# Attention and two expert layers on one core: the second batch's scores in one-head float32r tiles

## The chip, the cores and the metric

The kernel runs on one core of a Trainium2 chip. The metric is the device time of one execution in microseconds, as the median of the runs; three runs of the kernel before stand at 1053.46, 1054.71 and 1057.16 us. A core has TensorE (PE, which multiplies matrices; its weight loads are listed as PEld), VectorE (DVE), ScalarE (ACT), GpSimd (POOL) and SyncE (SP), which here issues all transfers. Each engine works through its own instructions in order.

## The reference

The inputs q, k and v have the shape 4 batches x 8 heads x 576 positions x 64. A query sees the keys of its own block of 64 positions and of earlier blocks:

```python
scores = scale * np.matmul(q, k.transpose(0, 1, 3, 2))
mask = block_i >= block_j
scores = np.where(mask, scores, -1000000000.0)
scores = scores - np.max(scores, axis=-1, keepdims=True)
attn = np.exp(scores)
attn = attn / (np.sum(attn, axis=-1, keepdims=True) + 1e-09)
return np.matmul(attn, v).astype(np.float32)
...
x = np.ascontiguousarray(attn_out.transpose(0, 2, 1, 3)).reshape(B * S, H * D)
a, b = x @ w_a, x @ w_b          # first layer, 2304 x 512 by 512 x 1536
x = a * b @ w_out
xn = x / np.sqrt(np.mean(x * x, axis=-1, keepdims=True) + 1e-06) * rms_g
g = xn @ w_gate                  # second layer
out = g / (1 + np.exp(-g)) * (xn @ w_val) @ w_out
```

The three weight matrices of each layer come as 64-bit floats and are turned into pairs of 32-bit numbers on the core.

## The kernel before, in words

The heads are worked in 16 pairs, m = 0 to 15, four pairs a batch. Each pair has two parts, its first six query blocks of 64 and its last three. In each part `score` makes the score tiles, their maximum (DVE, L480 to L484) and their exponential (ACT, L486), and then the scaling by the sum (POOL, L498). `p_transposes` turns the scaled tiles (PE L523; ACT L525 and DVE L529 take them out of PSUM), and `values` or, for the first batch, `whole_values` multiplies with v (PE L592 or L548).

There are two forms of score tile, chosen by `single(m)`. The old form takes 64 queries of both heads of a pair as 128 rows, against the keys of both heads, in plain float32 (L457, two recorded instructions for each). The new form (L465) takes 128 queries of one head. Query and key are split in a rounded part and a remainder, float32r; the keys' two parts lie above one another in the 128 rows, so one matmul with the rounded queries (`qh`) and one with their remainders (`ql`) do all the products. The last 64 queries of both heads share the tile `qe`. In that form `make_q` does the split (ACT L111 the rounding, POOL L121 the remainder), `make_k` scales and splits the keys (ACT L411, DVE L413), and a DVE memset (L467) masks a 64x64 corner of each tile. Before the change `SINGLE = 2`: pairs 8 to 15 (third and fourth batch) have the new form, pairs 0 to 7 the old one.

The buffers of the two forms overlap. The raw queries of the new form lie in the buffer of the old form's even pairs (`qz0`), the remainders in that of the odd pairs (`qz1`), and the rounded queries in the two `x` buffers of the weight decoding.

The first layer runs over blocks of 512, 256, 512 and 1024 tokens, the second over three blocks of 768. While the first block runs, the first layer's weights are decoded: a piece is loaded (SP L190), taken apart (ACT L146 and L149, DVE L152, POOL L153), and split in two float32r parts (ACT L111; DVE or POOL L121). Three of five pieces lie in the slots `ld`, two in `st`. Attention of the next batch runs beside each block of the first layer; how far it may go is set by the cost that each step yields, against that of the main products, times `PACE`. The scheduler of the framework then puts each engine's instructions in an order by priority and by its own forecast of times.

In the second layer each product is made from seven smaller ones over three blocks of the ring `w`; ACT copies of PSUM (L743, L862) stand between one product and the next. Beside a block runs the normalisation of the next one, `normed`: the load of x2 (L1006), its squares (ACT L1009 and L1011), the mean by a matmul with ones, the factors and the scaling (DVE L1044), then the sums and splits that the next block multiplies. `before_fc` advances it by one step for each of the 24 steps of a block.

Of the kernel before, what the change touches and what calls it, by code (L numbers as in the profile page):

```python
# [9 lines left out]
F32R = mybir.dt.float32r  # L10
# [6 lines left out]
P = 128  # L17
# [10 lines left out]

WHOLE = 1

SINGLE, MASKED = 2, -1e30

RING = 19
UNSCALE = 2.0 ** -8
# [17 lines left out]
def tile_attention_moe_moe(  # L52
# [15 lines left out]
    B, H, D, S = q.shape  # L68
# [22 lines left out]
    stage = staging.enter_context(tc.tile_pool(name="stage", bufs=2))  # L91
# [24 lines left out]
    def split(hi, lo, src, eng_hi, eng_lo, late=None):  # L116

        ins = copy(eng_hi, hi, src)
        if eng_hi is act and late is not None:
            behind(ins, late)  # L120
        eng_lo.tensor_tensor(lo, src, hi.bitcast(F32), ALU.subtract)  # L121
        return ins
# [34 lines left out]
    w_pieces = []  # L157
# [13 lines left out]
    LANDING, landing = 5, []  # L171
    staged, prepared, wtiles = {}, [0], {}

    def stage_loads(n):
        while len(staged) + prepared[0] < min(n, len(w_pieces)):
            i = len(staged) + prepared[0]
            layer, kind, f, y = w_pieces[i]
            if layer == 0 and i % LANDING < LANDING - 2:
                if not landing:
                    landing.append(stage.tile([P, LANDING - 2, 4 * P], I64, tag="bg", name="ld", bufs=1))  # L180
                st = landing[0][:, i % LANDING]
            else:
                st = stage.tile([P, 4 * P], I64, tag="st", name="st", bufs=2)
            if kind == "o" and layer == 1:

                for dm in range(KC):
                    z, o = divmod(dm * TF + f % TF, KC)
                    sp.dma_start(out=st[:, dm * P:dm * P + P], in_=w_o[1][f // TF, z, :, o * P:o * P + P])
            else:
                sp.dma_start(out=st, in_=(w_ab if kind == "ab" else w_o)[layer][f, y])  # L190
            staged[i] = st

    def prepare():

        i = prepared[0]
        if i >= len(w_pieces):
            return
        stage_loads(min(i + min(2 + i, LANDING), max(len(w_pieces) // 2, i + 2)))
        layer, kind, f, y = w_pieces[i]
        w = 4 * P  # L200
        if layer == 0:
            if y == 0:
                if kind == "ab":
                    wtiles["ab", f] = wab.tile([P, 4, KC * P], F32R, tag="ab", name="ab")
                else:
                    wtiles["o", f] = wop.tile([P, 2, TF * DM], F32R, tag="o", name="o")
            t = wtiles[kind, f]
            dst = t[:, 2 * y:2 * y + 2, :] if kind == "ab" else t[:, :, y * w:(y + 1) * w]
        else:
            if f % 2 == 0:  # L210
                quarters["src"] = stage.tile([P, 8, 2 * P], F32, tag="src", name="src", bufs=1)
            src = quarters["src"]
            if kind == "ab":
                at = (0, 6)[f % 2]
                place = src[:, at:at + 2, :]
            else:
                place = src[:, f % 2:f % 2 + 7:6, :]
            decode(staged.pop(i), place)
            prepared[0] += 1
            if f % 2 == 1:  # L220
                combine(wc_dram[f // 2][y] if kind == "ab" else wco_dram[f // 2], src)
            return
        x = decode(staged.pop(i)).rearrange("p a b -> p (a b)")
        prepared[0] += 1
        split(dst[:, 0, :], dst[:, 1, :], x, act, eng[W_LO[i % len(W_LO)]], "act")
        if y == (1 if kind == "ab" else TF - 1):
            sp.dma_start(out=wab_dram[f] if kind == "ab" else wo_dram[f], in_=t.bitcast(F32))
# [20 lines left out]
    def fetch_ab(n):  # L248
        t = wtiles["ab", n] = wab.tile([P, 4, KC * P], F32R, tag="ab", name="ab")
        sp.dma_start(out=t.bitcast(F32), in_=wab_dram[n])  # L250

    def fetch_o(i):
        t = wtiles["o", i] = wop.tile([P, 2, TF * DM], F32R, tag="o", name="o")
        sp.dma_start(out=t.bitcast(F32), in_=wo_dram[i])
# [55 lines left out]
    def attention(pools, x_of, done):  # L310
# [20 lines left out]
        MAIN = S - Q  # L331
        q_raw, q_hi, q_lo = {}, {}, {}

        FIRST_SINGLE = SINGLE * (H // 2)

        def single(m):
            return m >= FIRST_SINGLE
# [93 lines left out]
        def make_q(m, part):  # L431
            if m >= NP or not single(m):
                return
            if not q_hi:
                assert prepared[0] >= len(w_pieces) // 2
                for hh in range(2):
                    q_hi[hh] = stage.tile([P, MAIN], F32R, tag="x", name="qh", bufs=2)
                t = ap.tile([P, 2 * MAIN + 3 * Q], F32R, tag="qz1", name="ql")
                for hh in range(2):
                    q_lo[hh] = t[:, hh * MAIN:(hh + 1) * MAIN]  # L440
                for x, end in ((q_hi, ap.tile([P, 3 * Q], F32R, name="qe")), (q_lo, t[:, 2 * MAIN:])):
                    act.activation(end[:, Q:2 * Q], pp[NQ - 1][:, S:S + Q], AF.Copy)
                    x["end"] = end
            a, z = (PARTS[0][0] * Q, PARTS[0][-1] * Q + Q) if part == 0 else (PARTS[1][0] * Q, MAIN)
            todo = [(q_hi[hh][:, a:z], q_lo[hh][:, a:z], q_raw[m][:, hh, a:z]) for hh in range(2)]
            if part == 1:
                ends = [x["end"].rearrange("p (t q) -> p t q", t=3)[:, 0:3:2] for x in (q_hi, q_lo)]
                todo.append((*ends, q_raw[m][:, :, MAIN:]))
            for hi, lo, raw in todo:
                split(hi, lo, raw, act, pool)  # L450
            if part == 1:
                load_q(m + 1)
# [162 lines left out]
        for u in range(2 * NP + 2):  # L615
            m, part = divmod(u, 2)
            if u >= 2:
                yield from (whole_values if (u - 2) // H < WHOLE else values)(u - 2)
            sc = list(SCORED[part]) if m < NP else []
            ct = p_transposes(u - 1) if 1 <= u <= 2 * NP else iter(())  # L620
            if sc:
                yield score(m, sc.pop(0))
                if len(sc) > 2:
                    yield score(m, sc.pop(0))
                if part == 0:
                    make_vv(m)
                    make_q(m, 1)
                else:
                    make_k(m + 1)
                    if m + 1 > FIRST_SINGLE:  # L630
                        make_q(m + 1, 0)
            alive = True
            while sc or alive:
                c = next(ct, None) if alive else None
                if c is None:
                    alive = False
                else:
                    yield c
                if sc:
                    yield score(m, sc.pop(0))  # L640
            if m < NP and part == 1:
                if m + 1 == FIRST_SINGLE:
                    make_q(m + 1, 0)
                load(m + 2)

# [413 lines left out]
    for at, (layer, t0, n_tok, parts) in enumerate(blocks):  # L1059
# [10 lines left out]
        if layer == 0:  # L1070
            acc = [accs.tile([P, KC, BMAX[0]], F32, tag="acc", name="acc")]
            for o, n in parts[1:]:
                nxt.append(split_of(t0 + o, n, True))
                acc.append(xs.tile([P, KC, S], F32, tag="xf", name="acc", bufs=2))
                t = xs.tile([P, KC, S], F32R, tag="xf", name="h", bufs=2)
# [16 lines left out]
        def before_fc(fc, n_tiles=n_tiles, at=at, layer=layer, following=following, norm=norm, got=got):  # L1092
            if at == 0:
                if fc > 0:
                    for _ in range(TF):
                        if prepared[0] < len(w_pieces) // 2:
                            prepare()
            elif layer == 0:
                if fc % TF == 0:
                    fetch_o(fc // TF)  # L1100
                if fc + 2 < FC:
                    fetch_ab(fc + 2)
                n = sum(BACKGROUND[:at]) + min(BACKGROUND[at], BACKGROUND[at] * (fc + 1) // (FC - 3))
                while prepared[0] < len(w_pieces) // 2 + n:
                    prepare()
                if prepared[0] == len(w_pieces) and not rings:
                    staging.close()
                    rings.append(ctx.enter_context(tc.tile_pool(name="ring", bufs=RING, side="right")))
                    fetch_to(RING - 1)
            if following and following[0] == 0 and fc + 2 >= FC:  # L1110
                fetch_ab(fc + 2 - FC)
            if fc > 0:
                for _ in range(FC * 2 // n_tiles):
                    if layer == 0 and len(got.get("x") or ()) == len(EARLY):
                        break
                    got["x"] = next(norm, None) or got.get("x")
# [100 lines left out]
```

## Time and profile before

| | us |
|---|---|
| median of 3 runs | 1054.71 |
| the profiled execution | 1053.99 |
| its span, first to last instruction | 1052.0 |
| PE busy | 1037.8 |
| DVE busy | 702.6 |
| ACT busy | 619.0 |
| POOL busy | 423.5 |

The span is that of the profiled execution; the rest of its time lies before the first and behind the last instruction. A busy PE is not a PE at its peak: the recorded duration of a matmul reaches over the start of the next, so for the cost of one the distance between two starts is the better measure. Idle time counts only where it ends up on the path to the last instruction.

### The profile page before, as it was taken

The page shows a single profiled execution, that of the slowest core. Times are in us where ns is not written, and L with a number is a line of the kernel's source. Part 1 is how long each engine was busy: PE and PEld are TensorE (multiplying, and loading weights), DVE is VectorE, ACT ScalarE, POOL GpSimd, SP SyncE. Part 2 cuts the span into 40 slices and gives each one's busy share as a digit, 9 for nine tenths or more (in the row PEclk, how much of TensorE's full clock was granted, in tenths as well). Part 3 has the DMA queues.
Part 4 walks back from the last instruction along what each step waited for, and adds up shares of the span by engine and source line. Part 5 has one row for each costly group of instructions (what it writes and reads, how often), then busy time and mean ns, then how long its engine had stood idle before and what let it go on. Part 6 is the DMA issues. An engine that isn't in the chain of part 4 may idle for free.

```text
span 1052.0 us, 16959 instructions
## 1 busy us (share of the span) xinstructions
PE 1037.8 (99%) x5676; PEld 934.4 (89%) x5676; DVE 702.6 (67%) x1371; ACT 619.0 (59%) x1376; POOL 423.5 (40%) x448
## 2 busy tenths in 40 slices
PE   9989999999999999999999999999999999999998
PEld 6768877899998888888888888999999999999998
DVE  5546767677766777676687734784876838666285
ACT  7868968667656766556544323653656536355362
POOL 5855766546564655455554501120221202212020
PEclk9999999999999999999999999999999999999999
DMA  9865978889997765788989665787789888887883
GB/s 242 232 202 194 294 258 300 313 270 290 347 371 261 270 223 210 288 330 313 340 312 349 255 225 181 216 284 258 242 301 302 275 268 251 294 265 240 266 247 116
DMA packets 116380, 281.25 MB, mean 267 GB/s; under 512 B 27971, under 2 KB 40771, under 8 KB 105798
## 3 DMA queue, kind: packets, MB, share of 16 engines
q1 hardware_dynamic: 116294, 280.18, 79.8%
q8 instruction: 45, 0.74, 0.3%
q14 instruction: 41, 0.34, 0.1%
HBM read 218.77 MB, written 61.36 MB: 266 GB/s over the span
## 4 chain that ended last, share of the span: by engine, by line
PE 85%; ACT 4%; DMA 4%; DVE 2%; POOL 2%; SPq 1%; issue 1%; POOLq 0%; ACTq 0%
PE mm L735 25%; PE mm L766 12%; PE mm L707 8%; PE mm L708 8%; PE mm L709 8%; PE mm L667 4%; PE mm L668 4%; PE mm L669 4%; PE t L592 3%; PE t L523 3%; PE s L465 3%; PE t L548 1%; DMA st<-in_w_o_dram 1%; POOL x L153 1%; PE s L457 1%
## 5 line engine op out<-in xcount | busy, mean ns | idle before, releaser
L708 PE MATMUL mm<-xl,ab 128*128 128x512 f32 (+1 forms) x480 | 180.8, 377 | 0.0
L707 PE MATMUL mm<-xh,ab 128*128 128x512 f32 (+1 forms) x480 | 179.8, 377 | 0.0
L709 PE MATMUL mm<-xh,ab 128*128 128x512 f32 (+1 forms) x480 | 179.4, 374 | 0.0
L735 PE MATMUL mm<-hT,w 128*128 128x384 f32 x576 | 165.5, 337 | 1.3 <-ACT mm L743 1.3
L121 POOL TENSOR_TENSOR hl<-g,hh 128x384 fp32r<-128x384 f32 x36 | 42.7, 1186 | 298.7 <-ACT hh L111 298.7
L735 PE MATMUL mm<-hB,w 128*128 128x384 f32 x432 | 125.9, 336 | 0.0
L766 PE MATMUL mm<-hh,w 128*128 128x384 f32 x504 | 125.2, 336 | 0.0
L743 ACT ACTIVATE mm<-mm 128x384 f32<-128x384 f32 x144 | 66.8, 474 | 75.5 <-PE mm L735 39.3
L735 PEld LDWEIGHTS mm<-hT,w 128*128 128x128 f32 x576 | 105.9, 188 | 2.7 <-ACT mm L743 2.4
L709 PEld LDWEIGHTS mm<-xh,ab 128*128 128x128 f32 x480 | 90.5, 189 | 15.2 <-issue 0.5
L707 PEld LDWEIGHTS mm<-xh,ab 128*128 128x128 f32 x480 | 90.4, 188 | 15.1 <-issue 0.2
L708 PEld LDWEIGHTS mm<-xl,ab 128*128 128x128 f32 x480 | 90.5, 189 | 14.8 <-issue 0.2
L498 POOL TENSOR_SCALAR pp<-pp,st 128x256 f32<-128x256 f32 (+4 forms) x144 | 83.3, 592 | 50.0 <-DVE st L495 35.5
L735 PE MATMUL mm<-lT,w 128*128 128x384 f32 x288 | 96.9, 337 | 0.0
L486 ACT ACTIVATE pp<-s,st 128x288 f32<-128x288 f32 (+8 forms) x142 | 72.0, 510 | 33.0 <-DVE st L480 16.2
L766 PEld LDWEIGHTS mm<-hh,w 128*128 128x128 f32 x504 | 90.6, 188 | 0.3 <-ACT mm L743 0.3
L766 PE MATMUL mm<-hl,w 128*128 128x384 f32 x252 | 81.4, 336 | 0.0
L735 PEld LDWEIGHTS mm<-hB,w 128*128 128x128 f32 x432 | 79.5, 188 | 0.0
L667 PE MATMUL mm<-hh,o 128*128 128x512 f32 (+1 forms) x208 | 77.8, 375 | 1.2 <-DVE acc L677 0.7
L153 POOL TENSOR_TENSOR src<-src,st 128x512 uint32<-128x512 uint32 x36 | 47.8, 1328 | 74.0 <-DVE src L152 74.0
L668 PE MATMUL mm<-hh,o 128*128 128x512 f32 (+1 forms) x208 | 77.4, 373 | 0.0
L669 PE MATMUL mm<-hl,o 128*128 128x512 f32 (+1 forms) x208 | 75.3, 370 | 0.4 <-DVE hl L121 0.4
(161 smaller groups left out, 2453.4 us busy)
## 6 DMA issues: line engine op xcount, KB each, us to landing
w<-wc SPq DMA_DIRECT2D x252, 256.0 KB, 3.5
ab<-wab SPq DMA_DIRECT2D x36, 1024.0 KB, 7.9
w<-wco SPq DMA_DIRECT2D x126, 256.0 KB, 3.3
wc<-bg SPq DMA_DIRECT2D x12, 1792.0 KB, 8.3
o<-wo SPq DMA_DIRECT2D x12, 1536.0 KB, 8.0
st<-in_w_ab_dram SPq DMA_DIRECT2D x34, 512.0 KB, 5.7
wab<-ab SPq DMA_DIRECT2D x12, 1024.0 KB, 5.9
wco<-bg SPq DMA_DIRECT2D x6, 1792.0 KB, 6.6
```

The costliest lines, as they stand in the source:

```text
L153: pool.tensor_tensor(x, x, lo, ALU.add)
L486: act.activation(pi[:, a:z], pss[x][:, 0:z - a], AF.Exp, bias=s[:, b:b + 1], scale=1.0, accum_out=t3[:, b, x:x + 1],)
L498: pool.tensor_scalar(t, t, s[:, y:y + 1], 1.0, ALU.mult, ALU.mult)
L667: pe.matmul(ps[:, 0:n], wh, hh, start=(y == 0), stop=False)
L668: pe.matmul(ps[:, 0:n], wl, hh, start=False, stop=False)
L669: pe.matmul(ps[:, 0:n], wh, hl, start=False, stop=(y == TF - 1))
L707: pe.matmul(ps[:, 0:n], wh[:, a:z], xhc, start=(c == 0), stop=False)
L708: pe.matmul(ps[:, 0:n], wh[:, a:z], xlc, start=False, stop=False)
L709: pe.matmul(ps[:, 0:n], wl[:, a:z], xhc, start=False, stop=(c == KC - 1))
L735: pe.matmul(ps, lhs, rhs[:, c, :], start=(start and c == 0 and y == 0), stop=(c == 1 and y == 2), skip_group_check=not start,)
L743: act.activation(to, ps, AF.Copy)
L766: pe.matmul(banks[m], lhs, rhs, start=(start and f == group[0] and y == 0), stop=(f == group[-1] and y == 2), skip_group_check=not start,)
```

## The change

Three numbers are changed, and the code that the first one needs. `SINGLE` goes from 2 to 1, so that pairs 4 to 7, the second batch, get the new form of score tile. At pair 4 the decoding still needs its `x` buffers; the rounded queries therefore lie in the buffer `src` (that of the first pair's keys) for pairs 4 to 7 and move to the `x` buffers at pair 8. A weight piece's load is issued four pieces ahead of its decoding for five. In a block of the second layer the normalisation of the next block begins at step 3 for step 1.

```diff
-SINGLE, MASKED = 2, -1e30
+SINGLE, MASKED = 1, -1e30
...
-        stage_loads(min(i + min(2 + i, LANDING), max(len(w_pieces) // 2, i + 2)))
+        stage_loads(min(i + min(2 + i, LANDING - 1), max(len(w_pieces) // 2, i + 2)))
...
-            if not q_hi:
+            if part == 0 and m == 2 * (H // 2):
                 assert prepared[0] >= len(w_pieces) // 2
                 for hh in range(2):
                     q_hi[hh] = stage.tile([P, MAIN], F32R, tag="x", name="qh", bufs=2)
+            if not q_hi:
+                t = stage.tile([P, 2, MAIN], F32R, tag="src", name="qh", bufs=1)
+                for hh in range(2):
+                    q_hi[hh] = t[:, hh]
                 t = ap.tile([P, 2 * MAIN + 3 * Q], F32R, tag="qz1", name="ql")
...
-                    if m + 1 > FIRST_SINGLE:
+                    if m + 1 > FIRST_SINGLE and m + 1 != 2 * (H // 2):
                         make_q(m + 1, 0)
...
-                if m + 1 == FIRST_SINGLE:
+                if m + 1 in (FIRST_SINGLE, 2 * (H // 2)):
                     make_q(m + 1, 0)
...
-            if fc > 0:
+            if fc > 2 * layer:
```

From L435 on the lines of the changed kernel stand four lower than those of the kernel before.

PE, around the last score of pair 3 (`qz_145`, 512 wide) and the first ones of pair 4, before (`pp_150` to `pp_158` are the nine score tiles of a pair, `pw` their transposes):

```order
L457 MATMUL s<-ks,qz_145 128x512
L457 MATMUL s<-ks,qz_144 128x64
L523 MATMUL t<-ident,pp_154 128x128
...
L709 MATMUL mm<-xh,ab 128x512
L457 MATMUL s<-ks,qz_144 128x128
L457 MATMUL s<-ks,qz_144 128x192
L523 MATMUL t<-ident,pp_156 128x128
L457 MATMUL s<-ks,qz_144 128x256
L523 MATMUL t<-ident,pp_157 128x128
```

and of the changed kernel, the same place:

```order
L461 MATMUL s<-ks,qz_145 128x512
L469 MATMUL s<-ks,qh 128x128
L527 MATMUL t<-ident,pp_154 128x128
...
L711 MATMUL mm<-xh,ab 128x512 x3
L469 MATMUL s<-ks,ql 128x128
L712 MATMUL mm<-xl,ab 128x512
...
L469 MATMUL s<-ks,qh 128x256
L469 MATMUL s<-ks,ql 128x256
...
L469 MATMUL s<-ks,qh 128x384
L469 MATMUL s<-ks,ql 128x384
L527 MATMUL t<-ident,pp_156 128x128
```

Five tiles of pair 4 now stand ahead of the transposes of pair 3's last tiles; before, there were three.

POOL at the same place, before (`pp_158` is the last tile of pair 3, `vv<-vr` the split of v):

```order
L498 TENSOR_SCALAR pp_158<-pp_158,st 128x576
L114 TENSOR_SCALAR vv<-vr 128x10x64
L429 TENSOR_TENSOR vv<-vr,vv 128x10x64
L153 TENSOR_TENSOR x<-x,ld 128x512
L498 TENSOR_SCALAR pp_156<-pp_156,st 128x448
L498 TENSOR_SCALAR pp_157<-pp_157,st 128x512
```

and of the changed kernel:

```order
L502 TENSOR_SCALAR pp_158<-pp_158,st 128x576
L121 TENSOR_TENSOR ql<-qr,qh 128x384 x2
L121 TENSOR_TENSOR ql<-qr,qh 128x128 x2
L121 TENSOR_TENSOR ql<-qr,qe 128x2x64
L114 TENSOR_SCALAR vv<-vr 128x10x64
L153 TENSOR_TENSOR x<-x,ld 128x512
L429 TENSOR_TENSOR vv<-vr,vv 128x10x64
L502 TENSOR_SCALAR pp_156<-pp_156,st 128x448
L502 TENSOR_SCALAR pp_157<-pp_157,st 128x512
```

The five remainders of pair 4's queries have come in ahead of the split of v, and a piece of the weights (L153) stands between its two halves.

ACT at the switch from the first layer to the second, before (`hB` and `hT` are the splits of the new layer's first block):

```order
L111 ACTIVATE hB_6892<-xf 128x768
L111 ACTIVATE hT_6896<-T_6522 128x768
L1009 ACTIVATE sq<-xf 128x768
L1011 ACTIVATE y<-xf 128x768
L743 ACTIVATE mm<-mm 128x384
L1011 ACTIVATE y<-xf 128x768
L862 ACTIVATE p_7042<-mm 128x384
```

and of the changed kernel:

```order
L747 ACTIVATE mm<-mm 128x384
L866 ACTIVATE p_7183<-mm 128x384
L747 ACTIVATE mm<-mm 128x384 x2
L823 ACT_TABLE_LOAD
L823 ACTIVATE sig<-mm 128x384
L747 ACTIVATE mm<-mm 128x384
L823 ACTIVATE sig<-c_7228 128x384
L747 ACTIVATE mm<-mm 128x384
L823 ACTIVATE sig<-c_7242 128x384
L111 ACTIVATE hh<-g_7289 128x384
L1013 ACTIVATE sq<-xf 128x768
```

The square of the next block's x2 (L1009, now L1013) has moved from ahead of the layer's first copy to behind its sixth PSUM eviction.

## Rows read from the trace of the kernel before

**Rows 1.** Page, part 1: busy time, share and instructions of each engine.

```profile
PE 1037.8 (99%) x5676; PEld 934.4 (89%) x5676; DVE 702.6 (67%) x1371; ACT 619.0 (59%) x1376; POOL 423.5 (40%) x448
```

**Rows 2.** Windows: length, busy time of each engine, PE clock, DMA share, GB/s.

```profile
60.00:70.00 10.00, 7.95 (x35) 6.38 (x34) 2.80 (x10) 5.70 (x18) 6.67 (x9) 0.83 0.62 151
75.00:200.00 125.00, 121.05 (x611) 97.45 (x610) 90.69 (x185) 98.73 (x224) 80.69 (x78) 1.00 0.79 268
80.00:130.00 50.00, 50.00 (x255) 41.17 (x255) 36.26 (x74) 44.88 (x102) 32.77 (x31) 1.00 0.74 241
225.00:300.00 75.00, 75.00 (x618) 74.48 (x618) 57.80 (x158) 55.60 (x149) 45.13 (x58) 1.00 1.00 327
```

**Rows 3.** Timeline of PE: start, duration, line, tiles, count, idle before.

```profile
105.62 0.65 PE L457 MATMUL s<-ks,qz 128*128 128x288 f32 x2
106.11 0.27 PE L523 MATMUL t<-ident,pp 128*128 128x128 f32 x1
...
217.02 0.30 PE L465 MATMUL s<-ks,qe 128*128 128x288 f32 x1
...
218.09 0.39 PE L667 MATMUL mm<-hh,o 128*128 128x512 f32 x1
...
221.98 0.39 PE L465 MATMUL s<-ks,qh 128*128 128x512 f32 x1
...
222.92 0.28 PE L709 MATMUL mm<-xh,ab 128*128 128x256 f32 x1
...
227.88 0.22 PE L465 MATMUL s<-ks,qh 128*128 128x128 f32 x1
...
228.06 0.33 PE L707 MATMUL mm<-xh,ab 128*128 128x256 f32 x1
```

**Rows 4.** Groups by form: count, busy us, mean ns of one, idle before.

```profile
L111 ACT ACTIVATE qh<-qr 128x384 fp32r<-128x384 f32 x16 | 8.2, 521 | 5.4 <-POOL pp L498 2.4 <-PE s L465 1.1 <-DMA qr<-in_q_dram 1.0
L111 ACT ACTIVATE qh<-qr 128x128 fp32r<-128x128 f32 x16 | 4.7, 307 | 2.1 <-PE s L465 2.1
L411 ACT ACTIVATE ks<-kr 128x1152 fp32r<-128x1152 f32 x8 | 9.3, 1160 | 0.0
L420 ACT ACTIVATE ks<-kr 128x576 f32<-128x576 f32 x4 | 2.8, 702 | 0.0
L413 DVE SCALAR_TENSOR_TENSOR ks<-kr,ks 64x1152 fp32r<-64x1152 f32 x8 | 12.2, 1530 | 0.2
L467 DVE MEMSET s<- 64x64 f32 x64 | 7.1, 112 | 18.3 <-PE s L465 10.7 <-PE t L523 3.7 <-ACT ph L525 3.2
L121 POOL TENSOR_TENSOR ql<-qr,qh 128x384 fp32r<-128x384 f32 x16 | 16.1, 1011 | 9.0 <-ACT qh L111 9.0
L121 POOL TENSOR_TENSOR ql<-qr,qh 128x128 fp32r<-128x128 f32 x16 | 7.2, 461 | 3.5 <-PE mm L708 1.3 <-PE s L465 1.1 <-ACT qh L111 1.1
```

**Rows 5.** Timeline of POOL and PE at pair 4's first scores.

```profile
61.36 0.72 POOL L114 TENSOR_SCALAR vv<-vr 128x640 fp32r<-128x640 f32 x1 [4.31 <-DMA vr<-in_v_dram]
62.17 1.55 POOL L429 TENSOR_TENSOR vv<-vr,vv 128x640 fp32r<-128x640 f32 x1
...
62.93 0.71 PE L457 MATMUL s<-ks,qz 128*128 128x128 f32 x4
...
64.93 1.30 POOL L498 TENSOR_SCALAR pp<-pp,st 128x448 f32<-128x448 f32 x2
...
65.62 0.33 PE L523 MATMUL t<-ident,pp 128*128 128x128 f32 x1 [1.98 <-POOL pp L498]
```

**Rows 6.** Timeline of ACT and PE at the switch of layers.

```profile
651.74 0.84 ACT L1009 ACTIVATE sq<-xf 128x768 f32<-128x768 f32 x1 [14.45 <-DMA xf<-x_dram]
...
652.13 0.33 PE L735 MATMUL mm<-hB,w 128*128 128x384 f32 x1
...
653.23 0.47 ACT L743 ACTIVATE mm<-mm 128x384 f32<-128x384 f32 x1
...
653.75 0.44 PE L735 MATMUL mm<-hT,w 128*128 128x384 f32 x1 [1.29 <-ACT mm L743]
```

## The prediction

> **What bounds the kernel now.** I read the busy shares first, then the stages, then the single waits. TensorE is busy 99% of the span, every other engine below 70% [rows 1]. So work taken from TensorE shortens the kernel, unless TensorE then waits for something else. Where it could wait, the windows tell [rows 2]. In 225:300, where one-head score tiles already run beside the main products, PE is busy 75.00 of 75 us with ACT at 55.60, 74%. In 75:200, the first block, where the weights are still being decoded beside the second batch's attention, PE is busy 121.05 of 125, ACT 98.73 (79%), DVE 90.69, POOL 80.69, DMA share 0.79. Nothing but PE is full there on average; in 80:130 ACT is at 44.88 of 50. In 60:70 PE is busy only 7.95 of 10 and its granted clock averages 0.83. After 225 two places matter, the end of the first layer (below) and nothing else that the change touches.
>
> **The score products.** Four pairs of heads (second batch) change form. A busy PE row overlaps the next one, so I take the distance from one start to the next [rows 3]. Old form: a 128x288 tile, two recorded instructions, goes from 105.62 to 106.11, 0.49 us, 1.70 ns a column. A pair has 64, 128, ... 576 columns, 2,880 together: 4.90 us. New form: the last queries of both heads (8 matmuls of 288) take 217.02 to 218.09, 1.07 us; the two 512-wide tiles (4 matmuls) 221.98 to 222.92, 0.94; a 128-wide tile (2 matmuls) 227.88 to 228.06, 0.18, so two are 0.36; for the 256- and 384-wide tiles I use the 512's rate, 0.459 ns a column, 0.47 and 0.70. Sum 3.54 us. The gain is 1.36 us a pair, 5.4 us for four. Transposes and value products keep their columns and only change order.
>
> **What the other engines get for it** [rows 4]. Per pair ACT gets two 128x384 and three 128x128 roundings of q (2 x 0.521 + 3 x 0.307) and a 1.160 us k scaling for one of 0.702: 2.42 us. DVE gets the k remainder and eight mask memsets, 1.530 + 8 x 0.112 = 2.43 us. POOL gets the q remainders, 2 x 1.011 + 3 x 0.461 = 3.41 us. SP gets four q and k transfers for three, of twice the bytes together. I leave out four exponentials, reductions and scalings a pair that are 64 columns wider.
>
> Three of the four pairs fall into 75:200. ACT there goes from 98.73 to 106.0 of 125 us, 79% to 85%; DVE to 98, POOL to 91. What hides this is the idle time of these engines; what it costs without that cover I bound from two windows. The low end is 0: the same tiles run in 225:300 with no PE idle. The high end: PE idle was 0 at 74% ACT and 3.95 us at 79%, and carried on by the same slope to 85% it is 4.7 us more. The two stages differ by the weight decoding, so neither is nearer; I take the middle, 2.4 us lost again.
>
> **The switch itself, near 57 us.** The first pair of the new form needs its q remainders from POOL before its second matmul, and their buffer is free only after the last score of the pair before. In the order POOL now makes them just ahead of the value conversion L114. In the trace POOL sat idle 4.31 us before that L114, waiting for v, until 61.36 [rows 5]. The five remainders, 3.4 us, fit into that hole, so I cost them at nothing; without the hole the scalings at 64.93, and the transposes that wait for them at 65.62, come 3.4 us later. PE's own wait there (1.98 us before 65.62, after the two scores at 62.93) stays in my sum, as its cause, the late v, stays. Scores of this pair are filler in that wait, so part of its 1.36 us may buy nothing; that is inside the 2.4 us.
>
> **Weight loads four ahead.** The load of a piece still waits for the same slot, and on SP the first loads stand in the same places among the q, k and v loads. I take 0. The bounds are what one late transfer costs in this stage: POOL waited 4.31 us for v, 1.98 us of it reached PE [rows 5]; so between 2.0 us gained, if the load that now stands ahead of v comes out of its way, and 2.0 us lost, if one more comes late.
>
> **Later normalisation in the second layer.** At the layer switch ACT stands 14.45 us before its square L1009, which waits for x2 until 651.74; behind it in ACT's queue is the copy L743, which starts at 653.23, and PE, which had issued at 652.13, goes on only at 653.75 [rows 6]. Matmuls of this form follow each other in 0.17 to 0.18 us, so 1.4 us is lost. Now six ACT evictions of the new layer stand ahead of that square, the first of them this copy. By then x2 has landed, so I count the whole 1.4 us as gained. What is late next is the normalisation: its squares, row transfers and factors come two products-of-work later, but the splits that the next block needs keep their place among ACT's evictions, so nothing follows. The third block's square also moves, past the end of the block; no PE wait is recorded there, 0.
>
> **Sum.** -5.4 + 2.4 - 1.4 = -4.4 us. The profiled execution took 1053.99 us (span 1052.0), so 1049.6; the median of the runs shown is 0.7 us higher, so I forecast 1050.3 us for the median.
>
> **Rivals.**
> A, the forecast: PE's saving minus a partial return. With the return between 0 and 4.7 the time is 1047.9 to 1052.6.
> B, slower: ACT becomes the bound of the first block. Place: 80:130, where ACT has 5.1 us idle and gets two pairs, 4.8 us. Point from which it decides: if that idle is waiting for DVE and POOL, which also get more work, and not spare time, the 4.8 us are added to ACT's queue; the evictions of the main products stand in it, and PE's saving then only lengthens PE's waits. Price +4.8 - 1.4: 1058.1. For it: DVE, POOL and the transfers grow too. Against it: PE was busy 50.00 of 50 us in 80:130, with ACT at 90% there.
> C, the scores buy nothing: the first block ends when the weights are decoded and the second batch is normalised, whatever PE does. Only the layer switch counts: 1053.3. For it: PE's idle 3.95 us in 75:200. Against it: 97% busy.
> D, more than the forecast: the wait near 63 us goes too. In the new order POOL decodes the next weight piece ahead of the second half of the value conversion, 1.55 us earlier, ACT and the scores behind it follow, and more of the new pair stands before the transposes. Price: the 1.98 us, and the clock. In 60:70 it averaged 0.83 of 2.4 GHz, as stretches at 1.2 GHz give, worth 10 x 0.17 = 1.7 us. With no return in the first block: 1054.7 - 5.4 - 1.4 - 3.7 = 1044.2; with 2.4, 1046.6. Against it: v is still loaded behind the same weight pieces on SP.
> On that clock: the row shows the mean 0.83 in the very window in which PE waited. The Trainium skill, "TensorE: Matmul & The Clock Gate", section "What's actually happening", says that half rate is the array's default and that sustained activity releases it; the trace agrees. By that rule a second wait of this size, at the new switch, would cost its length and again some 1.7 us, which would move the sum from 1050.3 to 1054.0; by the rows alone, which show PE's clock at 1.00 through the waits of 75:200, it costs its length only. By that rule I keep a little more chance on no change.
>
> **Chances.** A 0.53, C 0.23, B 0.13, D 0.11. About 0.3% (3.2 us) is what a measurement of this kernel can tell from no change: below 1051.5 is faster, above 1057.9 slower. Of A some 0.42 lies below 1051.5, all of D does; C and the rest of A are no change; B, at 1058.1, counts as slower: faster 0.53, same 0.34, slower 0.13. The range reaches down between D's two prices, takes in 2.0 us either way for the loads, and ends at B: 1045.5 to 1058. The likeliest case's own range is 1047.9 to 1052.6.
>
> **What would show it.** Right: score matmuls of the new form in the first block at the distances above; PE's wait at the layer switch gone and L743 ahead of L1009; ACT at about 85% between 75 us and the first block's end, which comes 2 to 5 us earlier. Wrong: PE idle above 8.7 us in that stage (B, C); a POOL wait for the q remainders ahead of L114, or no half-clock stretch near 65 us (D). A wait of PE at the start of a later second-layer block would show that the normalisation now comes too late, which I exclude.

## The result, and the profile after

The change made the kernel slower: 1071.22 us median of 6 runs (1068.47 to 1074.78), against 1054.56 (1052.89 to 1059.7) for the kernel before on the same chip; ratio 1.015, 95% interval 1.0123 to 1.0178. The profiled execution took 1069.92 us, span 1068.1, 16.1 us more than before. The forecast was 1050.3, with a range that ended at 1058.

Page of the kernel after, part 1 (columns as in [rows 1]):

```profile
PE 1042.5 (98%) x5692; PEld 941.2 (88%) x5692; DVE 713.4 (67%) x1407; ACT 625.6 (59%) x1396; POOL 440.1 (41%) x468
```

The added work of the other engines is near the forecast over the whole program (DVE +10.8 us for 9.7, ACT +6.6 for 9.7, POOL +16.6 for 13.6). It does not bound anything by its amount: all of them stay far below PE. The windows say where PE stood still. Those of after, columns as in [rows 2]; the second and the third answer to rows there:

```profile
50.00:75.00 25.00, 22.27 (x103) 16.34 (x102) 14.89 (x37) 18.16 (x48) 19.17 (x23) 0.93 0.59 179
75.00:200.00 125.00, 118.47 (x619) 99.69 (x618) 98.99 (x209) 103.43 (x235) 86.16 (x91) 0.97 0.78 261
80.00:130.00 50.00, 49.89 (x265) 42.57 (x265) 39.06 (x83) 43.37 (x98) 33.98 (x36) 1.00 0.77 248
150.00:200.00 50.00, 44.51 (x222) 36.78 (x221) 40.02 (x80) 41.22 (x90) 32.45 (x34) 0.93 0.76 255
300.00:325.00 25.00, 20.98 (x128) 19.29 (x128) 18.00 (x44) 13.89 (x37) 15.54 (x20) 0.86 0.86 292
700.00:725.00 25.00, 22.63 (x119) 21.82 (x118) 14.08 (x23) 10.04 (x23) 3.30 (x3) 0.93 0.73 218
812.00:862.00 50.00, 46.27 (x261) 44.67 (x260) 34.21 (x66) 27.22 (x58) 9.76 (x8) 1.00 0.76 235
```

and the last four of the kernel before, which were not shown:

```profile
150.00:200.00 50.00, 47.80 (x243) 38.63 (x242) 38.14 (x73) 39.75 (x89) 33.59 (x33) 1.00 0.82 284
300.00:325.00 25.00, 24.19 (x154) 21.69 (x153) 16.77 (x43) 13.63 (x38) 13.14 (x19) 1.00 0.94 330
700.00:725.00 25.00, 24.97 (x144) 24.65 (x143) 9.06 (x15) 9.65 (x22) 1.02 (x1) 1.00 0.79 252
812.00:862.00 50.00, 50.00 (x290) 50.00 (x289) 29.18 (x49) 23.93 (x53) 7.99 (x6) 1.00 0.84 265
```

Four places lose PE time: the end of the first block, the change of blocks at 300 to 325, and two in the second layer. In three of them the clock falls too. Below, PE's *stall* is the time from one matmul's start to the next, less what matmuls of that width usually take, summed over a stretch; it holds waits and half-clock matmuls alike. From before to after it goes from 5.9 to 7.1 us in 50:100, 6.2 to 11.6 in 100:200, 1.5 to 6.2 in 300:312, 2.0 to 1.4 in 650:662, 1.0 to 5.3 in 687:725 and 0.8 to 5.8 in 812:862. That is +20.0; less the 5.3 us of score work that PE really saved, it gives +14.7 of the 16.1. Each count is of one execution: e3 and e12 below, whose engines have the same order up to 304 us, differ by 2.1 us in 100:200, so a difference of 2 us between two such counts tells nothing.

**Second layer.** Timeline of after around 705 us, SP's queue (SPq), DVE, ACT and PE, each in order of time (start, duration, engine, line, tiles, count; idle before it and what ended it):

```profile
698.73 0.32 SPq L1041 DMA_DIRECT2D row<-sm  x1
...
700.34 0.32 SPq L1043 DMA_DIRECT2D y<-row  x1
...
702.09 0.55 DVE L830 SCALAR_TENSOR_TENSOR g<-mm,asb 128x384 f32<-128x384 f32 x1
...
705.27 1.02 DVE L1048 SCALAR_TENSOR_TENSOR xf<-xf,rms_g,y 128x768 f32<-128x768 f32 x1 [2.64 <-DMA y<-row]
706.21 0.55 DVE L885 TENSOR_TENSOR c<-p,mm 128x384 f32<-128x384 f32 x1
...
707.14 1.02 DVE L830 SCALAR_TENSOR_TENSOR g<-c,asb 128x384 f32<-128x384 f32 x2
...
707.72 0.52 ACT L111 ACTIVATE hh<-g 128x384 fp32r<-128x384 f32 x1 [4.15 <-DVE g L830]
...
709.36 1.27 PE L770 MATMUL mm<-hh,w 128*128 128x384 f32 x4 [2.05 <-ACT hh L111]
```

L1048 (L1044 before) scales x for the *next* block by y. It stands in DVE's row ahead of the gate products of the *current* group, and waits for y, whose load SP issued at 700.34. The gate products, ACT's rounding and PE's matmul queue up behind it. In 812:862 the same scaling does it again, through a copy of ACT (the profile names a load of w as what DVE waited for; y's own load was issued at 839.95):

```profile
845.18 1.02 DVE L1048 SCALAR_TENSOR_TENSOR xf<-xf,rms_g,y 128x768 f32<-128x768 f32 x1 [4.91 <-DMA w<-wco]
...
846.75 0.47 ACT L747 ACTIVATE mm<-mm 128x384 f32<-128x384 f32 x1 [5.18 <-DVE c L885]
...
847.28 0.62 PE L770 MATMUL mm<-hh,w 128*128 128x384 f32 x2 [1.88 <-ACT mm L747]
```

PE also waits 0.43 us at 831 and 1.09 at 834 for copies of ACT; in ACT's row a square root and two table loads stand ahead of them, as in e5 below.

**Change of blocks at 304 to 310.** DVE and PE of after:

```profile
304.98 2.11 DVE L413 SCALAR_TENSOR_TENSOR ks<-kr,ks 64x1152 fp32r<-64x1152 f32 x1
...
307.50 0.56 DVE L602 TENSOR_TENSOR xf<-t,xf 64x384 f32<-64x384 f32 x1
...
308.29 0.55 DVE L602 TENSOR_TENSOR xf<-t,xf 64x384 f32<-64x384 f32 x1
...
309.16 0.41 DVE L121 TENSOR_TENSOR hl<-mm,hh 128x256 fp32r<-128x256 f32 x1
...
305.85 0.39 PE L671 MATMUL mm<-hh,o 128*128 128x256 f32 x1 [0.99 <-ACT hh L111]
...
309.62 0.80 PE L673 MATMUL mm<-hl,o 128*128 128x256 f32 x2 [3.03 <-DVE hl L121]
```

The remainder hl, for which PE waits, stands behind attention's k remainder and value sums. After the wait two 256-column matmuls take 0.80 us; before, such pairs took 0.50.

**End of the first block.** POOL, DVE, ACT and PE of after:

```profile
172.92 1.28 POOL L121 TENSOR_TENSOR ab<-x,ab 128x512 fp32r<-128x512 f32 x1
...
174.24 1.49 DVE L152 TENSOR_SCALAR x<-a 128x512 uint32<-128x512 uint32 x1 [1.36 <-POOL ab L121]
...
175.98 0.68 DVE L719 SCALAR_TENSOR_TENSOR mm<-mm,asb 128x512 f32<-128x512 f32 x1
...
175.76 0.68 ACT L149 ACTIVATE a<-ld 128x512 f32<-128x512 f32 x1 [1.49 <-DVE x L152]
...
177.34 0.58 ACT L111 ACTIVATE hh<-mm 128x512 fp32r<-128x512 f32 x1
...
177.98 0.80 PE L671 MATMUL mm<-hh,o 128*128 128x512 f32 x1 [3.20 <-ACT hh L111]
```

A decoding step (L152) waits for its buffer, held by POOL; the gate product and the rounding that PE needs stand behind it on DVE and ACT.

### The profile page after: what moved, and what is told of

The parts are those of the page before. It is cut to its first block, busy times and chain, and to the rows that moved or that the text cites. A ratio compares the mean times of both kernels' runs of the same rounds, so it can differ in the third digit from the quotient of the medians.

```text
span 1068.1 us, 17111 instructions
## 1 busy us (share of the span) xinstructions
PE 1042.5 (98%) x5692; PEld 941.2 (88%) x5692; DVE 713.4 (67%) x1407; ACT 625.6 (59%) x1396; POOL 440.1 (41%) x468
## 3 DMA queue, kind: packets, MB, share of 16 engines
HBM read 221.13 MB, written 61.36 MB: 264 GB/s over the span
## 4 chain that ended last, share of the span: by engine, by line
PE 84%; DVE 6%; ACT 4%; DMA 3%; POOL 2%; issue 1%; ACTq 0%; DVEq 0%; POOLq 0%; SPq 0%
PE mm L739 21%; PE mm L770 11%; PE mm L711 9%; PE mm L712 8%; PE mm L713 8%; PE mm L671 5%; PE mm L673 5%; PE mm L672 4%; PE t L596 3%; PE t L527 3%; PE s L469 3%; PE t L552 1%; DMA y<-row 1%; DVE ks L413 1%; PE s L461 1%
## 5 line engine op out<-in xcount | busy, mean ns | idle before, releaser
L770 PE MATMUL mm<-hh,w 128*128 128x384 f32 x504 | 127.6, 340 | 4.1 <-ACT mm L747 2.1
L711 PEld LDWEIGHTS mm<-xh,ab 128*128 128x128 f32 x480 | 90.3, 188 | 16.1 <-DVE xh L113 0.6
L712 PEld LDWEIGHTS mm<-xl,ab 128*128 128x128 f32 x480 | 90.4, 188 | 14.7
L153 POOL TENSOR_TENSOR src<-src,st 128x512 uint32<-128x512 uint32 x36 | 47.1, 1308 | 66.1 <-DVE src L152 52.1
```

Source lines behind the costliest of these rows:

```text
L153: pool.tensor_tensor(x, x, lo, ALU.add)
L711: pe.matmul(ps[:, 0:n], wh[:, a:z], xhc, start=(c == 0), stop=False)
L712: pe.matmul(ps[:, 0:n], wh[:, a:z], xlc, start=False, stop=False)
L770: pe.matmul(banks[m], lhs, rhs, start=(start and f == group[0] and y == 0), stop=(f == group[-1] and y == 2), skip_group_check=not start,)
```

## Experiments

Unless a base is named, a kernel is the one before with the edit shown. Ratios are to the kernel before, run beside it.

**The three parts apart.** Four kernels. e2 and e4 each put one line of the change into the kernel before:

```diff
-            if fc > 0:
+            if fc > 2 * layer:
...
-        stage_loads(min(i + min(2 + i, LANDING), max(len(w_pieces) // 2, i + 2)))
+        stage_loads(min(i + min(2 + i, LANDING - 1), max(len(w_pieces) // 2, i + 2)))
```

e1 is the changed kernel with the first of these taken back, e3 with both taken back, so that only the scores are left.

> The changed kernel with one edit taken back: the second layer's normalisation starts with the first product group again, instead of the third. Theory N (late normalisation): its row transfer now lands about 26 us later after each block start, the scaling that waits for it stands in the vector engine's queue ahead of the gate products, and PE loses 4.3 us near 705 and 5.0 near 824 to 857. Then this kernel is 8 to 9.5 us faster than the changed one, about 1062, with the layer-switch wait of 1.3 us back near 653. Rival R (the second layer only follows what the first layer shifted): the two late stalls stay, and the time is within 2 us of 1071.

> The kernel before with only the later start of the second layer's normalisation. Theory N: 8 to 9.5 us slower than before, about 1063, with PE waits of 4 to 5 us in each of the first two second-layer blocks, some 45 us after the layer switch. Rival R: those waits need the first layer's shift too; then only the layer-switch gain of 0.6 to 1.4 us is seen, about 1053.5.

> The kernel before with only the second batch's scores in the one-head form; weight loads five ahead, normalisation early. Theory S (the scores' roundings and remainders cost more than PE saves): the stalls at the end of the first block (11.6 us in 100 to 200 for 6.2) and at 304 to 310 (6.2 us for 1.45) stay, 6 to 8 us slower than before, about 1061. Rival L (the later loads make those stalls): they go, and PE's 5.3 us of saving shows: about 1050.

> The kernel before with only the weight loads four pieces ahead for five. Theory S: no change, 1053 to 1056. Rival L: the first block loses 5 us or more, 1060 or above.

| kernel | median us | ratio | 95% interval |
|---|---|---|---|
| scores and loads (e1) | 1061.95 | 1.0081 | 1.0060 to 1.0101 |
| late normalisation (e2) | 1062.66 | 1.0079 | 1.0066 to 1.0092 |
| scores (e3) | 1062.46 | 1.0079 | 1.0066 to 1.0093 |
| loads (e4) | 1054.99 | 1.0007 | 0.9995 to 1.0020 |

Theory N holds, and so does S as to where the loss lies: the stalls stay with the scores alone. Whether the scores' work makes them, as S says, or their order is the question further down. Rivals R and L fall. The parts add up: 1.0079 x 1.0079 x 1.0007 is 1.0166 against 1.015. Scores and normalisation cost 8.3 us each, the loads nothing that can be told. In e1 PE is busy 24.97 of 25 us in 700:725 and 50.00 of 50 in 812:862.

**Why the late normalisation costs.** Two kernels on e2: e5 (first edit) puts the first scaling one step later, e6 (second edit) starts one group later still.

```diff
-        for _ in range(3):
+        for _ in range(3 + 1):
...
-            if fc > 2 * layer:
+            if fc > 3 * layer:
```

> The late normalisation alone (as in the second run), with four steps for three between the load of the row of factors y and the first scaling by it. On the vector engine the first scaling then stands 14 rows behind the last factor instead of 6, as in the kernel before (15). Theory P (place): PE's two waits of 3.7 us come from that one scaling standing ahead of the gate products before y has landed; with the later place they go: 1053 to 1055, that is 8 us below the late normalisation alone. Rival T (too late): the normalisation as a whole comes too late for the next block, and one step more makes it later still: 1062 or above.

> The kernel before with the second layer's normalisation begun one product group later still than in the change (the fourth group instead of the third). By the order of the vector engine the first scaling then falls 12 rows behind the last factor, not 6. Theory P (place): no wait on y, 1053 to 1055. Rival T (too late): more than 8 us slower than before, 1063 to 1068.

e5: 1056.48 us, 1.0012 (1.0000 to 1.0024); e6: 1058.42, 1.0033 (1.0023 to 1.0044). Theory P holds: starting *later* than the change is 0.46% faster than the change's own start, since the scaling then falls behind y's landing. Both stand above the 1053 to 1055 expected, by 1.5 and 3.4 us, and the windows show what is left (PE busy, the second number):

```profile
700.00:725.00 25.00, 25.00 (x144) 24.81 (x143) 12.07 (x19) 10.15 (x23) 2.37 (x3) 1.00 0.86 292
812.00:862.00 50.00, 47.90 (x273) 46.95 (x272) 26.18 (x51) 24.98 (x53) 7.49 (x6) 1.00 0.76 239
```

These are e5's. The wait near 700 is gone; in 812:862 2.1 us stay. There ACT's square root stands in its row until its input lands, with the copy that PE needs behind it; the second wait, 1.08 us at 826.86, follows the table load back for the next sigmoid (1.28 us at 824.23):

```profile
820.42 1.28 ACT L1031 ACT_TABLE_LOAD   x1
822.77 0.21 ACT L1031 ACTIVATE sm<-sm 128x6 f32<-128x6 f32 x1 [1.07 <-DMA sm<-row]
822.89 0.47 ACT L743 ACTIVATE mm<-mm 128x384 f32<-128x384 f32 x1
...
823.41 0.45 PE L735 MATMUL mm<-hT,w 128*128 128x384 f32 x1 [0.89 <-ACT mm L743]
```

In e6 the third kind: PE's own sum of the squares, in PE's row, waits for them.

```profile
678.02 0.62 PE L1023 MATMUL mm<-sh,ones_r 128*128 128x384 f32 x2 [2.38 <-ACT sh L111]
```

So each place in the normalisation that waits for a transfer or another engine can fall ahead of main work; which one does depends on the start.

**Why the scores cost: work or order.** On e3, e7 (first edit) leaves out the q remainders of three pairs, and e8 (second edit: 0.46), e10 (0.43) and e11 (0.50) change only the pace of attention in the first block. e9, e15 and e14 give the kernel before, the old form, the same three paces.

```diff
+                if m // (H // 2) == SINGLE and m > FIRST_SINGLE:
+                    copy(act, hi, raw)
+                    continue
                 split(hi, lo, raw, act, pool)
...
-PACE, AHEAD = (0.49, 1.0, 0.6), (50, 200, 200)
+PACE, AHEAD = (0.46, 1.0, 0.6), (50, 200, 200)
```

> The scores part alone (third run), but the q remainders of the second batch's last three pairs are left out: the products read the first pair's remainders again. It takes 3.4 us a pair from GpSimd and no product from PE; from about a third into the first block on PE's order is the same as in the third run, the stretches of both stalls included. Theory W (added work): the stalls between 150 and 185 us, 6.4 us more than before, come from GpSimd's queue being fuller and shrink to under 3 us more; about 1057.5. Theory O (order): they come from where decoding, attention and evictions now stand in each other's queues, and stay: 1060.5 to 1063. The stall of 5.5 us at 304 to 310 stays by both, as that block has the same work as before.

> The scores part alone with the first block's attention paced at 0.46 of the main products' spending instead of 0.49; the amount of work is the same on every engine. Theory O (order): the two stalls depend on the phase between attention and main products; the sum of PE's stalls in 50 to 325 us (18.5 us there) changes by 3 us or more, and the 5.5 us at 304 to 310, in a block whose own pace is unchanged, is among what changes: 1054 to 1059, or above 1065. Theory W (added work): the same amount of work, the same stalls, 1061 to 1064.

> The kernel before, old scores, with the first block's attention paced at 0.46 for 0.49, as in the paced run of the scores. That run stood 9 us below the scores part alone. Theory O (order, and phase against the new form): the slower pace takes away stalls that the scores' new form made and the old form did not have, so here it gains nothing: 1052 to 1059. Rival P (the pace is simply better): it gives its 9 us here too: 1044 to 1048.

> The scores part alone with the first block's attention paced at 0.43 (0.49 gave 1062, 0.46 gave 1054). Theory D (density: the other engines get too full when attention runs ahead): slower pace again no worse: 1050 to 1055. Theory O (order: stalls come and go with what stands next to what, without a trend): anywhere from 1052 to 1064, with stalls of several us in other places than at 0.46.

> The scores part alone with the first block's attention paced at 0.50, one step above the change's 0.49; the work is the same. Theory D (density): 1061 to 1065, as at 0.49 or a little worse. Theory O (order): a step of two per cent is enough to move stalls of several us; the waits at 174 to 178 and at 304 to 310 need not be there, and the time lies anywhere from 1053 to 1066.

> The kernel before with the first block's attention paced at 0.50 for 0.49. Theory F (the old form leaves slack, the new form none): the step changes little, 1052 to 1056. Theory O (any form is at the mercy of the order): it may lose or gain several us, up to 1062.

> The kernel before paced at 0.43. Theory F: 1051 to 1056, so that the old form's four paces lie within 4 us where the new form's lie within 9. Theory O: a spread as wide as the new form's, with one of the old form's paces 5 us or more above 1054.

| pace | old form, ratio | new form, ratio |
|---|---|---|
| 0.43 | 1.0063 (1.0047 to 1.0079) | 1.0018 (1.0005 to 1.0032) |
| 0.46 | 0.9982 (0.9971 to 0.9993) | 0.9987 (0.9978 to 0.9997) |
| 0.49 | 1 | 1.0079 (1.0066 to 1.0093) |
| 0.50 | 1.0002 (0.9990 to 1.0015) | 1.0007 (0.9998 to 1.0016) |

e7 gave 1057.63 us, 1.0023 (1.0013 to 1.0033).

The same work at a pace of 0.50 for 0.49 is 0.72%, 7.6 us, faster: the excess at 0.49 over 0.50 is order, not amount. Theory W's 1061 to 1064 for e8 falls with 1053.72, and so does rival P's 1044 to 1048 for e9 with 1052.41: the slower pace is not simply better. Theory O, order, fits all six paces (e8 lies 0.3 us under its range). PE's stall in 50:325 is 26.2 us in e3 by the count above (the 18.5 in e8's expectation was summed wrongly), 18.6 in e8, 14.8 before. No trend with the pace: theory D falls with 0.50, and theory F with the old form at 0.43, whose spread of 0.8% is nearly as wide as the new form's 0.9%. What settles the place at 304 to 310 is that row of e15, the *old* scores at 0.43:

```profile
303.72 2.11 DVE L413 SCALAR_TENSOR_TENSOR ks<-kr,ks 64x1152 fp32r<-64x1152 f32 x1
...
304.60 0.39 PE L667 MATMUL mm<-hh,o 128*128 128x256 f32 x1 [0.99 <-ACT hh L111]
...
308.36 0.79 PE L669 MATMUL mm<-hl,o 128*128 128x256 f32 x2 [3.03 <-DVE hl L121]
```

and its window:

```profile
300.00:325.00 25.00, 20.98 (x122) 19.34 (x121) 16.82 (x40) 12.98 (x38) 15.19 (x19) 0.86 0.84 279
```

The same two waits, 0.99 and 3.03 us, the same busy time and clock as in the changed kernel, without any of its code. From 278 us on PE, DVE, ACT and POOL have the same order in e15 as in e3. The new form does not make this stall; it shifted the rows into the arrangement, the order of the streams on each engine, that has it. e7 fits: it does different work before 200 us but has e3's order again from 258 us on, and its 300:325 shows 20.99 and 0.86 again, while 150:200, from which it takes work, goes to 50.00 of 50 us. So at this pace the stall at the end of the first block does need the remainders, and e7's time is the 1057.5 of theory W, not the 1060.5 to 1063 of theory O. Yet it is no clean win for theory W: the order moved too, and e7 has a new stall of 4.7 us in 200:225.

**One row of DVE.** e12, on e3, leaves out the k remainder of pair 13, the one at 304:

```diff
-dve.scalar_tensor_tensor(low, raw[D:P], SCALE, low.bitcast(F32), ALU.mult, ALU.subtract)
+if m != 13:
+    dve.scalar_tensor_tensor(low, raw[D:P], SCALE, low.bitcast(F32), ALU.mult, ALU.subtract)
```

> The scores part alone, with the remainder of one pair's k left out, the one that VectorE makes at 304 us, 2.11 us there (the products of that pair then use the rounded k twice). The order of every engine up to that place is the same. Theory V (row of VectorE): PE's 3.2 us wait for hl near 305 us is hl standing behind this remainder and the value sums in VectorE's row; without it the wait is 1 to 1.7 us and the stalls of 300 to 325 us fall from 7.4 to 4 to 5.5: about 1060. Rival G (GpSimd or ScalarE decide): the wait stays above 2.8 us, 1062.

1058.24 us, 1.0037 (1.0022 to 1.0052). The 3.03 us wait for hl is gone from the trace altogether, more than the 2.11 us removed, and the clock of the window stays at 1.00 (PE's timeline, then the window):

```profile
308.40 0.39 PE L672 MATMUL mm<-hh,o 128*128 128x256 f32 x1 [0.99 <-ACT hh L111]
```

```profile
300.00:325.00 25.00, 23.84 (x164) 21.78 (x163) 18.06 (x50) 17.09 (x47) 17.54 (x24) 1.00 1.02 358
```

Theory V holds in direction; leaving out this row also changed the order behind this place, so the whole 4 us is not that one row's.

**What remains of the scores' saving.** e13, on e8 (new form, pace 0.46), leaves out the q remainders as e7 does and, by the edit below, the k remainders of the same pairs. e16 is the changed kernel with a pace of 0.46 (e8) and range(3 + 1) (e5).

```diff
-                dve.scalar_tensor_tensor(low, raw[D:P], SCALE, low.bitcast(F32), ALU.mult, ALU.subtract)
+                if m // (H // 2) != SINGLE or m == FIRST_SINGLE:
+                    dve.scalar_tensor_tensor(low, raw[D:P], SCALE, low.bitcast(F32), ALU.mult, ALU.subtract)
```

> The paced scores (0.46), with the q and k remainders of the second batch's last three pairs left out: 3.4 us of GpSimd and 1.5 us of VectorE a pair less, the same products on PE. Theory W (the added work returns what PE saves): 3 to 6 us below the paced run, 1048 to 1051. Theory O (it is the order alone): within 2 us of the paced run, 1052 to 1056.

> The whole change with its two late places mended: the first block's attention paced at 0.46, and four steps for three ahead of the scaling by y. By the sum of the single runs (0.9987 for the paced scores, 1.0012 for the mended normalisation, 1.0007 for the loads) 1.0006, about 1054 to 1057. If the parts do not add up, because each moves the order of the others, it stands more than 4 us from that.

e13: 1049.60 us, 0.9949 (0.9931 to 0.9966), 4 us below e8; its stall in 50:325 is 13.1 for 18.6. e16: 1056.09, 1.0013 (1.0001 to 1.0026): the parts still add up, and the mended change is no better than before. At 0.46 and 0.50, where neither form stands at its worst, they are within 0.05% of each other: PE's 5.3 us come back as stalls. By the count above the new form has 5.8 us more of them in 50:325 at 0.46 (e8 against e9) and 3.9 more at 0.50 (e11 against e14). e13 speaks for the remainders on POOL and DVE as the reason, as theory W has it, but taking them away also moves the order, and a step of pace moves as much; I count it as likely, not as shown.

**The layer switch.** e17, on e9, and e18, on e8, put the squares behind the copies L743:

```diff
-            act.activation(to, ps, AF.Copy)
+            gate["copy"] = act.activation(to, ps, AF.Copy)
...
-        behind(act.activation(sq, x[:, 0, :], AF.Square), "hh")
+        square = act.activation(sq, x[:, 0, :], AF.Square)
+        behind(square, "hh")
+        behind(square, "copy")
...
-            act.activation(y, x[:, c, :], AF.Square)
+            behind(act.activation(y, x[:, c, :], AF.Square), "copy")
```

> Old scores, pace 0.46, normalisation begun as early as before, but its squares stand behind the copies that ScalarE makes for the new layer's first group, and the first scaling by y still 12 and 14 rows behind the last factor. Theory Q (the first copy waits behind both squares): PE's wait of 1.3 us near 653 goes and none comes in its place; 1.0 to 1.5 us below the same kernel without it (0.9982), about 0.997 of before, 1051. Rival: a later step waits for the squares instead (PE's sums of the squares), no gain or a loss up to 3 us.

> New scores, pace 0.46, squares behind the copies. By Theory Q 1.0 to 1.5 us below the paced scores (0.9987), about 0.9975 of before; the difference to the old scores stays within 2 us either way, since the added work returns what PE saves.

e17: 1052.08 us, 0.9983 (0.9968 to 0.9998); e18: 1054.52, 1.0003 (0.9992 to 1.0014). No gain over 0.9982 and 0.9987: theory Q falls. (e18 stands 0.16% above e8, and 2.1 us above e17, a little more than expected. Up to 652 us PE, DVE, ACT and POOL have the same order in e18 and e8, yet e18's profiled execution has 2.4 us more stall in 50:325; the cause stays open.) ACT and PE of e17:

```profile
647.62 0.47 ACT L743 ACTIVATE mm<-mm 128x384 f32<-128x384 f32 x1 [13.09 <-PE mm L735]
652.08 0.49 ACT L862 ACTIVATE p<-mm 128x384 f32<-128x384 f32 x1 [3.98 <-DMA x_dram<-acc]
652.47 0.86 ACT L743 ACTIVATE mm<-mm 128x384 f32<-128x384 f32 x2
...
653.01 0.44 PE L735 MATMUL mm<-hT,w 128*128 128x384 f32 x1 [1.19 <-ACT mm L743]
```

The first copy now runs at once, but the next instruction of ACT, L862, waits 3.98 us for the store of the first layer's result, and the second copy stands behind it. The wait moved by one row. e9 (pace alone, 0.9982) and e17 are the fastest complete kernels here, 0.2% below the kernel before.

## Why the prediction was wrong

- **"The splits that the next block needs keep their place among ACT's evictions, so nothing follows."** This step failed, and cost 8.3 us. I looked at who needs the normalisation (the next block, far away) and not at who stands *behind* its waiting instructions on DVE and ACT. The wait of PE that I excluded came in both blocks: 2.05 us at 709 and 1.88 at 847 behind the scaling by y, and 1.09 at 834 behind the square root.
- **"So I count the whole 1.4 us as gained."** PE's interval there went from 1.62 us (652.13 to 653.75 in [rows 6]) to 1.09 (659.18 to 660.27 after): 0.5 us. I took L1009 for the only square in front; L1015 (L1011 before) kept its place ahead of the copy and still waited for x2, which had not landed as I said it would, and e17 shows a wait for the store right behind it. The rows of after:

```profile
659.00 0.84 ACT L1015 ACTIVATE y<-xf 128x768 f32<-128x768 f32 x1 [14.64 <-DMA xf<-x_dram]
659.75 0.47 ACT L747 ACTIVATE mm<-mm 128x384 f32<-128x384 f32 x1
...
660.27 0.44 PE L739 MATMUL mm<-hT,w 128*128 128x384 f32 x1 [0.76 <-ACT mm L747]
```

- **The score products, -5.4.** Right: PE's score work fell by 5.3 us.
- **"I take the middle, 2.4 us lost again."** This step failed too. At good paces the return is the whole saving, the 4.7 us of my upper end and a little more; at the change's own pace it is about 14. The amounts were near (75:200 after: ACT 103.43 of 125 for the 106.0 forecast, DVE 98.99 for 98, POOL 86.16 for 91). What failed is reading a return off an engine's average share: the losses are single waits of 3 us where an instruction that PE needs stands behind another stream's. Rival B had the sign but not the place: 80:130 shows PE at 49.89 of 50 and ACT at 43.37.
- **Nothing about 300 to 325.** That block's work is unchanged, so I gave it no term. It took 4.7 us of the loss. The range had no term for a changed order either, though the same program at two paces differs by 8 us.
- **"The five remainders, 3.4 us, fit into that hole."** Not quite: they ran from 58.51 to 63.45, 4.9 us, so L114 came at 63.45 for 61.36. PE's wait there is 2.32 us for 1.98, now for an exponential of ACT, and another 0.34 before the transposes. A cost of some tenths.
- **Loads, 0.** Right (e4, and e1 against e3).
- **The clock.** In 300:312 PE waits 4.0 us (0.99 and 3.03) but stalls 6.2: most of the rest is matmuls at 1.2 GHz behind the wait. At 309.62 two of 256 columns take 0.80 us, and at 177.98 one of 512 takes 0.80 for the 0.39 of [rows 3]. The granted clock averaged 0.86 in 300:325, 0.93 in 150:200 and in 700:725, and stayed at 1.00 in 812:862. Right behind the three waits it was, in the kernel after:

```profile
178.00:182.00 4.00, 4.00 (x13) 3.29 (x14) 4.00 (x7) 2.19 (x5) 4.00 (x5) 0.50 0.87 330
309.60:312.00 2.40, 2.38 (x11) 2.38 (x12) 1.55 (x5) 0.28 (x2) 2.40 (x4) 0.50 0.84 267
709.40:714.00 4.60, 4.60 (x18) 4.60 (x19) 4.60 (x7) 2.13 (x5) 1.21 (x2) 0.63 0.62 187
```

I had kept the price of a wait to its length. Yet not every wait pays more. In e2 PE waits longer at the same place, and the clock stays at 1.00 in 700:725:

```profile
704.40 0.97 PE L766 MATMUL mm<-hh,w 128*128 128x384 f32 x4 [3.56 <-ACT hh L111]
```

The Trainium skill, "TensorE: Matmul & The Clock Gate", section "What's actually happening", has half rate as the default that activity releases, as weighed in the prediction; three of the four new places agree with it. By it the sum should have had such a price as a possible term, not as a certain one for each wait.
- **What was to show it.** PE's idle time in 75:200 is 6.5 us (125 less 118.47), below the 8.7 that I had set as the mark of failure, though the stage lost more than it gained: half-clock matmuls count as busy (4.00 of 4.00 us in 178:182 above, at a clock of 0.50), so the mark missed them. The first block's first result is stored at 216.94 us for 216.19, not 2 to 5 us earlier.

## What to carry to other kernels

Where several streams share in-order engines, ask of a moved instruction not only when its result is needed but what it waits for and which urgent instruction of another stream stands behind it. An instruction that waits for a transfer should stand on its engine's row only where the transfer has landed: one step more room (e5) took back most of what starting later had cost. Before a gain of half a per cent is credited to an edit, run the old and the new form at two or three neighbouring paces: here one notch moved either form by 0.8 to 0.9%.

## What the runs showed of the hardware

- The k remainder L413 took 1.36 us in the kernel after each of the six times that POOL stood still beside it. Beside work of POOL it took 1.75 to 2.17 us five times, 2.11 at 304 among them, and 1.36 once (at 253.51); the 1.53 of [rows 4] is a mean over both kinds. The Trainium skill, "GPSIMD Engine Reference", section "1. Specifications", says that GpSimd shares its SBUF interfaces with VectorE and contends with its instructions of two SBUF inputs; L413 is one, and the trace agrees in five of six cases.
- The two small transfers through HBM that carry the factors are slow for their size: the row written at 698.73 lets the load of y be issued at 700.34, and the scaling starts only at 705.27, 6.5 us for a row of 768 numbers. The Trainium skill, "DMA: Bandwidth & Descriptors", section "Anatomy of one DMA — SWDGE (gpsimd) path", gives some 2.0 us of fixed cost for a transfer issued by GpSimd. These go through SP: the write is near it (1.6 us to the next issue), the broadcast took 4.9 to the start of the scaling, in a window with a DMA share of 0.73.
